# Chunked delta rule with two heads in one TensorE instruction, one Gram product for k and q, and transposed 16-blocks brought by transfer

## The chip, the cores and the metric

The kernel runs on one core of a Trainium2 chip. The metric is the device time of one execution in microseconds (us); several runs give a median.

## The reference

```python
# q, k, v: (4, 8, 768, 48) fp32, beta: (4, 8, 768); 32 heads in all
k_n = k / (norm(k) + 1e-6)
for t in range(768):
    y[:, :, t] = einsum('bhd,bhde->bhe', q[:, :, t], state)
    v_old = einsum('bhde,bhd->bhe', state, kt)
    state = state + bt * einsum('bhd,bhe->bhde', kt, vt - v_old)
x = y.transpose(0, 2, 1, 3).reshape(3072, 384)
logits = x @ w_gate                      # 8 experts, the best one for each token
# softmax weight of that expert; each expert keeps its 80 heaviest tokens
out[tok] = gate_w[tok] * (relu(x[tok] @ w1[e]) @ w2[e])   # F = 1024, all fp32
```

## The kernel before

Time is cut into NC = 12 chunks of C = 64 steps. Within a chunk the recurrence is a triangular system: the Gram matrix of the normalized k, masked and scaled by beta, gives `B1`; its inverse is built from 16x16 blocks (solved on POOL by `solve`) that `merge_*` joins to 32 and then 64. The 32 heads are named by e (0, 1), p (0, 1) and g (0 to 7).

A loop over j from -4 to 11 is a software pipeline written out by hand: an iteration works on chunk j+4 (scaling k), j+3 (transposes, Gram products, `fetch`, `solve`), j+2 (`spread`, `merge_y16`, `merge_p2`), j+1 (the other merges) and j (the chain over the state: `chain_ks`, `chain_tr`, `chain_qs`, `chain_ku`, `chain_pu`, then `out_t` and `logits`). The order of the calls in the loop is the order on every engine and on every DMA queue. `fill(n)` puts n small VectorE instructions (Newton steps of the norm, the gate, the top 80) between.

PE products of 32 heads go through `tiles` and `mm`: each head is its own product on a 64x64 quarter of the array, and the order goes round the four quarters. In fp32 each product is two LDWEIGHTS/MATMUL pairs in the trace, so such a product of all heads is 64 pairs. Three PSUM buffers (`mtile`, two banks each) go round; `S_ps` holds the state for the whole loop.

`gram_k` leaves `B1`, which goes to `a_blocks` in DRAM and comes back (`fetch`) as diagonal 16-blocks, one block to a partition, for `solve`. Its result goes to `inv_blocks` and comes back through `spread` in eight small DMAs into `xe`. `merge_y16` transposes it on PE by a product with `eye`. The DMA of `a_blocks` and `fetch` are issued from ACT's queue, all others of the loop from SP's.

After the loop come the routing (threshold, ranks, lists of tokens) and the experts: for each of 8 experts a gather of 80 rows, products at L803 and L811, and a scatter. The expert weights are loaded after the loop.

Of the kernel before, what the change touches and what calls it, by code (L numbers as in the profile page):

```python
# [24 lines left out]
def kernel(  # L25
# [49 lines left out]
    i_dram = [nc.dram_tensor(f"inv_blocks{i}", (128, 256), F32, kind="Internal") for i in range(2)]  # L75
# [61 lines left out]
    beta_t = keep.tile([128, NC, 2, NQ], F32, name="beta_t")  # L137
    beta_u = keep.tile([128, NC, 2, NQ], F32, name="beta_u")
# [18 lines left out]
    with ExitStack() as actx:  # L157
# [19 lines left out]
        KTs, QTs, PTs, B1s, Y16s, P2s, Ys, NTs, bms, Xss, xs = ({} for _ in range(11))  # L177
        St = [None]
# [7 lines left out]
        def sq4(t):  # L186
            return t.rearrange("r b (g w) -> r b g w", w=64)

        def d48(t):
            return t[:, :, : NQ * D].rearrange("r b (g d) -> r b g d", d=D)  # L190

        def halves(fn):
            for n in range(2):
                fn(slice(4 * n, 4 * n + 4))

        def wide(m):
            return m.unsqueeze(1).unsqueeze(1).to_broadcast([128, 2, 4, 64])

        def row(g):
            return g // 2 % 2  # L200

        def grp(g):
            return g // 4 * 2 + g % 2

        HEADS = [(e, p, g) for e in range(2) for p in range(2) for g in range(NQ)]

        def tiles(where, emit):

            cls = {}
            for hd in HEADS:  # L210
                cls.setdefault(where(*hd), []).append(hd)
            order = [kk for kk in ((0, 0), (1, 1), (0, 1), (1, 0)) if kk in cls]
            for n in range(max(len(x) for x in cls.values())):
                for kk in order:
                    if n < len(cls[kk]):
                        emit(*cls[kk][n])

        def mm(out, lhsT, rhs, acc=False):
            if acc:
                nc.tensor.matmul(out, lhsT=lhsT, rhs=rhs, start=False, stop=False, skip_group_check=True)  # L220
            else:
                nc.tensor.matmul(out, lhsT=lhsT, rhs=rhs, start=True, stop=True)  # L222
# [13 lines left out]
        def load_k(c):  # L236
            if ok(c):
                kr[c] = inp.tile([128, NB, D], F32, name="kr", bufs=4)
# [10 lines left out]
        def load_v(c):  # L249
            if ok(c):  # L250
                vin[c] = inp.tile([128, 2, NQ, D], F32, name="vin")
                src = vf.rearrange("(q p e) (c t) d -> p e c t q d", p=2, e=2, t=C)
                for p in range(2):
                    for e in range(2):
                        nc.sync.dma_start(vin[c][hs(e ^ p), p], src[p, e, c])
# [46 lines left out]
        def beta_mask(c):  # L302
            if ok(c):
                bms[c] = mat.tile([128, 2, NQ, 64], F32, name="bm", bufs=2)
                nc.gpsimd.tensor_tensor(out=bms[c].rearrange("r p g w -> r (p g) w"),
                                        in0=beta_t[:, c].rearrange("r p g -> r (p g)").unsqueeze(2).to_broadcast([128, NB, 64]),
                                        in1=neg_strict.unsqueeze(1).to_broadcast([128, NB, 64]), op=Alu.mult)

        def trans(dst, src):
            pt = mtile()  # L310
            for g in range(NQ):
                nc.tensor.transpose(pt[:, g // 4, (g % 4) * 128 : (g % 4) * 128 + 128],  # L312
                                    src[:, 2 * g : 2 * g + 2, :].rearrange("r p d -> r (p d)"), ident)
            for n in range(2):
                nc.scalar.copy(dst[:, 4 * n : 4 * n + 4], pt[:, n].rearrange("r (g w) -> r g w", w=128))  # L315

        def trans_k(c):
            if ok(c):
                KTs[c] = mat.tile([128, NQ, 128], F32, name="KT")
                trans(KTs[c], kn[c % NKB])  # L320

        def trans_q(c):
            if ok(c):
                QTs[c] = mat.tile([128, NQ, 128], F32, name="QT")
                trans(QTs[c], qn[c % NQB])

        def gram(dst, KT, r, mul):
            ps = mtile()
            tiles(lambda e, p, g: (p, e),
                  lambda e, p, g: mm(ps[hs(e), p, 64 * g : 64 * g + 64], KT[hs(p, D), g, hs(e)], r[hs(p, D), g, hs(e)]))  # L330
            halves(lambda s: nc.vector.tensor_tensor(out=dst[:, :, s], in0=sq4(ps)[:, :, s], in1=mul(s), op=Alu.mult))  # L331

        def gram_k(c):
            if ok(c):
                B1 = B1s[c] = mat.tile([128, 2, NQ, 64], F32, name="B1")
                bm = bms.pop(c)
                gram(B1, KTs[c], KTs[c], lambda s: bm[:, :, s])
                ad = a_dram[c % 2].rearrange("(e g z) -> e g z", e=2, g=NB)
                for e in range(2):
                    nc.scalar.dma_start(ad[e, :, : 64 * 64].rearrange("g (r w) -> r g w", w=64),  # L340
                                        B1[hs(e)].rearrange("r p g w -> r (p g) w"))

        def gram_q(c):
            if ok(c):
                PTs[c] = mat.tile([128, 2, NQ, 64], F32, name="PT")
                gram(PTs[c], KTs[c], QTs[c], lambda s: wide(strict))
# [7 lines left out]
        def solve(c):  # L354
# [3 lines left out]
            X = Xss[c] = sml.tile([128, 16, 16], F32, name="Xs")  # L358
            nc.gpsimd.tensor_tensor(out=X, in0=NT.rearrange("p s t -> p t s"), in1=eye16, op=Alu.add)  # L359
            for t in range(14, 0, -1):  # L360
# [5 lines left out]
                nc.gpsimd.tensor_tensor(out=X[:, t + 1 :, 0:t], in0=X[:, t + 1 :, 0:t], in1=tv, op=Alu.add)  # L366

        def spread(c):
            if not ok(c):
                return  # L370
            nc.sync.dma_start(i_dram[c % 2][:, :], Xss.pop(c).rearrange("p c s -> p (c s)"))
            src = i_dram[c % 2].rearrange("(e g i) (c s) -> e i c g s", e=2, i=4, s=16)
            dst = xe[c % 2].rearrange("r p g w -> r (p g) w")
            for e in range(2):
                for i in range(4):
                    nc.sync.dma_start(dst[64 * e + 16 * i : 64 * e + 16 * i + 16, :, 16 * i : 16 * i + 16], src[e, i])

# [465 lines left out]
```

## Time and profile before

| | |
|---|---|
| three runs | 557.03 us median, 550.74 to 561.35 |
| profiled execution | 548.66 us, its span 546.6 us |
| mean granted TensorE clock | 0.824 |
| busy shares | PE 69%, PEld 60%, DVE 38%, ACT 22%, POOL 32% |

The profile is of one execution. Engines are PE (matmul), PEld (weight load, overlaps PE), DVE, ACT, POOL; SPq and ACTq are the queues from which DMAs are issued. In groups of instructions, "busy" is the time in which at least one instruction of the group ran, so busy time over count is the pace of a stream, while "mean ns of one" holds the latency of each and is longer. A wait put down to "issue" is one in which the engine waited for nothing that the profile shows.

### The profile page before, as it was taken

How to read it: one execution, taken by the hardware profiler on the slowest of the kernel's cores; microseconds unless marked ns; L12 is line 12 of the kernel's file. 1: busy time of each engine (PE TensorE's matmuls, PEld its weight loads, DVE VectorE, ACT ScalarE, POOL GpSimd, SP SyncE). 2: the span in 40 equal slices, each digit the busy share in tenths (PEclk: the TensorE clock that was granted, in tenths of full speed). 3: DMA queues.
4: the chain of work that ended last, by engine and by line, in shares of the span. 5: the costliest groups of instructions: out<-in, count | busy, mean ns of one | idle time of the engine just before them, and what ended most of it. 6: DMA issues, size and time to landing. Idle time of an engine off the chain costs nothing. (4 is left out here: it accounts for less than half of the span.)

```text
span 546.6 us, 24604 instructions
## 1 busy us (share of the span) xinstructions
PE 379.9 (69%) x11259; PEld 327.2 (60%) x11271; DVE 209.9 (38%) x557; ACT 121.4 (22%) x218; POOL 177.0 (32%) x464
## 2 busy tenths in 40 slices
PE   2454768787787767678878868787500139999996
PEld 2343657676766657567768757776400028787673
DVE  4551244222532456323565523365285820101010
ACT  2021333222423223222322333223100000000000
POOL 7458374426171526317171515110020050010010
PEclk9999797778788797878786897787855555999999
DMA  9665557545372816435362534131386982782000
GB/s 159 93 104 86 100 101 124 103 83 131 59 157 53 147 34 130 89 68 114 55 135 34 117 62 102 24 92 27 83 326 227 387 288 96 268 287 89 10 9 19
DMA packets 173063, 63.84 MB, mean 117 GB/s; under 512 B 155008, under 2 KB 167808, under 8 KB 172960
## 3 DMA queue, kind: packets, MB, share of 16 engines
q1 hardware_dynamic: 122016, 52.33, 39.1%
q10 hardware_dynamic: 50176, 7.98, 8.6%
q0 software_dynamic: 768, 1.97, 1.2%
q8 instruction: 88, 1.44, 1.1%
q14 instruction: 15, 0.12, 0.1%
HBM read 43.95 MB, written 18.28 MB: 114 GB/s over the span
## 5 line engine op out<-in xcount | busy, mean ns | idle before, releaser
L222 PE MATMUL pm<-Y,P 64*64 64x64 f32 x1536 | 49.7, 247 | 5.5 <-issue 5.4
L222 PEld LDWEIGHTS pm<-Y,P 64*64 64x64 f32 x1536 | 46.3, 161 | 9.2 <-issue 7.5
L364 POOL TENSOR_TENSOR tmp<-Xs,NT 128x14 f32<-128x14 f32 (+6 forms) x168 | 47.5, 283 | 13.2
L803 PEld LDWEIGHTS hp<-xTe,w 128*128 128x128 f32 x384 | 48.9, 209 | 2.5 <-issue 1.2
L366 POOL TENSOR_TENSOR Xs<-Xs,tmp 128x14 f32<-128x14 f32 (+6 forms) x168 | 45.0, 268 | 13.2
L803 PE MATMUL hp<-xTe,w 128*128 128x80 f32 x384 | 48.9, 293 | 0.1
L299 POOL TENSOR_TENSOR kn<-kr,inv 128x768 f32<-128x768 f32 x12 | 18.4, 1531 | 84.3 <-PE S_ps L220 81.3
L811 PE MATMUL yp<-w,hT 128*80 128x384 f32 x128 | 44.3, 501 | 0.0
L806 ACT ACTIVATE hT<-hp 128x320 f32<-128x320 f32 x16 | 7.0, 437 | 135.0 <-PE hp L803 135.0
L815 POOL DMA_INDIRECT out_dram<-y,idx_s x8 | 7.4, 920 | 85.1 <-DVE y L814 85.1
L359 POOL TENSOR_TENSOR Xs<-NT,eye 128x256 f32<-128x256 f32 x12 | 10.2, 850 | 72.7 <-DMA NT<-a_blocks 72.7
L461 DVE TENSOR_TENSOR U<-pm,beta_u 128x384 f32<-128x384 f32 x24 | 12.3, 552 | 53.6 <-PE pm L222 53.6
L811 PEld LDWEIGHTS yp<-w,hT 128*80 128x80 f32 x128 | 19.2, 156 | 20.4 <-issue 20.4
L331 DVE TENSOR_TENSOR PT<-pm,strict 128x512 f32<-128x512 f32 x24 | 15.4, 685 | 40.6 <-PE pm L222 40.6
L222 PE MATMUL pm<-U,PT 64*64 64x48 f32 x768 | 19.0, 246 | 14.6 <-issue 13.9
L315 ACT COPY KT<-pm 128x512 f32<-128x512 f32 x24 | 12.9, 589 | 71.4 <-PE pm L312 71.4
L394 DVE TENSOR_TENSOR P<-pm,mask 128x512 f32<-128x512 f32 x24 | 15.5, 686 | 31.6 <-PE pm L220 31.6
L410 ACT COPY Y<-pm 128x512 f32<-128x512 f32 x24 | 12.9, 589 | 62.8 <-PE pm L222 16.5
L814 DVE TENSOR_SCALAR y<-yp,gw_t 80x384 f32<-80x384 f32 x8 | 4.9, 614 | 55.5 <-PE yp L811 55.5
L222 PEld LDWEIGHTS pm<-U,PT 64*64 64x64 f32 x768 | 16.4, 158 | 16.3 <-issue 14.9
L222 PE MATMUL pm<-KT 48*64 48x64 f32 x768 | 20.4, 270 | 7.1 <-issue 5.7
L222 PEld LDWEIGHTS pm<-KT 48*64 48x64 f32 x768 | 18.7, 183 | 8.3 <-issue 6.2
(168 smaller groups left out, 725.6 us busy)
## 6 DMA issues: line engine op xcount, KB each, us to landing
w<-in_moe_w_dram SPq DMA_DIRECT2D x16, 1536.0 KB, 8.7
a_blocks<-B ACTq DMA_DIRECT2D x24, 256.0 KB, 4.7
vin<-in_v_dram SPq DMA_DIRECT2D x52, 96.0 KB, 4.0
kr<-in_k_dram SPq DMA_DIRECT2D x24, 192.0 KB, 4.0
qn<-in_q_dram SPq DMA_DIRECT2D x24, 192.0 KB, 5.4
x_rows<-x SPq DMA_DIRECT2D x24, 192.0 KB, 3.1
out_dram<-zero SPq DMA_DIRECT2D x12, 384.0 KB, 3.2
NT<-a_blocks ACTq DMA_DIRECT2D x12, 128.0 KB, 2.9
```

Of the source, the lines that this page charges most:

```text
L222: nc.tensor.matmul(out, lhsT=lhsT, rhs=rhs, start=True, stop=True)
L299: nc.gpsimd.tensor_tensor(out=kn[c % NKB][:, :, 0:D], in0=kr.pop(c), in1=inv.pop(c).unsqueeze(2).to_broadcast([128, NB, D]), op=Alu.mult)
L315: nc.scalar.copy(dst[:, 4 * n : 4 * n + 4], pt[:, n].rearrange("r (g w) -> r g w", w=128))
L331: halves(lambda s: nc.vector.tensor_tensor(out=dst[:, :, s], in0=sq4(ps)[:, :, s], in1=mul(s), op=Alu.mult))
L359: nc.gpsimd.tensor_tensor(out=X, in0=NT.rearrange("p s t -> p t s"), in1=eye16, op=Alu.add)
L364: nc.gpsimd.tensor_tensor(out=tv, in0=X[:, t + 1 :, t : t + 1].to_broadcast(sh), in1=NT[:, 0:t, t].unsqueeze(1).to_broadcast(sh), op=Alu.mult)
L366: nc.gpsimd.tensor_tensor(out=X[:, t + 1 :, 0:t], in0=X[:, t + 1 :, 0:t], in1=tv, op=Alu.add)
L394: halves(lambda s: nc.vector.tensor_tensor(out=P2[:, :, s], in0=sq4(ps)[:, :, s], in1=wide(mask), op=Alu.mult))
L410: halves(lambda s: nc.scalar.copy(Y4[:, :, s], sq4(ps)[:, :, s]))
L461: halves(lambda s: nc.vector.tensor_tensor(out=U[:, :, s], in0=d48(ps)[:, :, s], in1=beta_u[:, c, :, s].unsqueeze(3).to_broadcast([128, 2, ...
L803: nc.tensor.matmul(hp[:, (f - f0) * cap : (f - f0 + 1) * cap], lhsT=w1_t[:, c, f * 128 : (f + 1) * 128], rhs=xTs[e][:, c, :], start=(c == ...
L811: nc.tensor.matmul(yp[:cap, :DM], lhsT=hT[:, f, :], rhs=w2_t[:, f, :], start=(f == 0), stop=(f == FK - 1))
```

## The change

The heads are re-paired. Six products (`chain_ks`, `chain_qs`, `chain_ku`, `chain_pu`, `merge_p2`, `merge_y4`) take two heads in one instruction: the left sides of two heads are stacked on 128 partitions, the right side is a block-diagonal tile that holds both heads (`SB`, `UB`, `XB`, `YB`, zeroed once), and the two results stand side by side. Such a product is 32 pairs, of 128 rows, 64 weight columns (48 in `chain_ku`) and 128 or 96 moving columns, on the two column halves of the array in turn. `gram_k` and `gram_q` become one product with k^T as weights and k^T and q^T side by side as the moving side (64 pairs of 128 columns). `merge_y16` is gone: POOL writes the transposed blocks beside the blocks, and eight more small DMAs (`spread_t`, four from SP's queue, four from ACT's) bring them into `YB`. `chain_qs` and `chain_pu` accumulate in one PSUM tile, which ACT copies out; the DVE addition is gone. `vin` comes in two DMAs in place of four. `logits` uses 64 columns of weights in place of 32 (24 pairs in place of 48). `merge_y5` now goes round four quarters of the array in place of two. `kn` has five buffers in place of four, and the loop's order changes. The core of the diff:

```diff
-        NKB, NQB = 4, 2
+        NKB, NQB = 5, 2
...
-        xe = [blk.tile([128, 2, NQ, 64], F32, name=f"xe{i}") for i in range(2)]
+        XB = blk.tile([128, NB, 2, 64], F32, name="XB")
+        YB = blk.tile([128, NB, 2, 64], F32, name="YB")
+        SB = blk.tile([128, NQ, 2, 2, D], F32, name="SB")
+        UB = blk.tile([128, NB, 2, D], F32, name="UB")
...
+        PAIRS = [(a, 4 * c + ql) for a in range(2) for ql in range(4) for c in range(2)]
+        XPAIRS = [(a, 4 * c + 2 * r + q) for a in range(2) for c in range(2) for q in range(2) for r in range(2)]
...
+        def gram(c):
...
+            for h in range(2):
+                ps = mtile()
+                tiles(lambda e, p, g: (p, e),
+                      lambda e, p, g: mm(ps[hs(e), p, 128 * (g % 4) : 128 * (g % 4) + 128].rearrange("r (k w) -> r k w", k=2),
+                                         KQ[hs(p, D), g, 0, hs(e)], KQ[hs(p, D), g, :, hs(e)]),
+                      [hd for hd in HEADS if hd[2] // 4 == h])
...
+                nc.vector.tensor_tensor(out=own(B1), in0=pv[:, 0], in1=own(bm), op=Alu.mult)
+                nc.vector.tensor_tensor(out=own(PT), in0=pv[:, 1], in1=strict.unsqueeze(1).to_broadcast([128, 8, 64]), op=Alu.mult)
...
+            nc.gpsimd.tensor_copy(XY[:, 1], X.rearrange("p t s -> p s t"))
...
+        def spread_t(c, q):
...
+                    if h == q:
+                        eng = (nc.sync, nc.scalar)[q]
+                        eng.dma_start(YB[r : r + 16, :, h, 16 * i : 16 * i + 16], src[h, i, 1])
...
+                for p, g in PAIRS:
+                    mm(ps[hs(g // 4), p, 128 * (g % 4) : 128 * (g % 4) + 128].rearrange("r (e w) -> r e w", e=2),
+                       B1[:, slot(p, g)], XB[:, slot(p, g)], acc=True)
...
+                            mm(ps[hs(p), e, 128 * ql : 128 * ql + 128].rearrange("r (c w) -> r c w", c=2),
+                               P2[:, p, ql, e], YB[:, 8 * e + 4 * p + ql])
...
+                for e, g in PAIRS:
+                    mm(ps[hs(g // 4), e, 2 * D * (g % 4) : 2 * D * (g % 4) + 2 * D].rearrange("r (p d) -> r p d", p=2),
+                       KQ[:, g, 0, hs(e)], SB[:, g, e])
...
+                for e, g in XPAIRS:
+                    mm(pxs[c][hs(g % 4 // 2), g // 4, 4 * D * (g % 2) : 4 * D * (g % 2) + 4 * D]
+                       .rearrange("r (p e d) -> r e p d", p=2, e=2)[:, e], KQ[:, g, 1, hs(e)], SB[:, g, e],
+                       acc=e + g % 2 > 0)
...
+                        mm(S_ps[hs(p, D), g // 4, 2 * D * (g % 4) : 2 * D * (g % 4) + 2 * D].rearrange("r (e d) -> r e d", e=2),
+                           kb[:, 2 * g + p, 0:D], UB[:, slot(p, g)], acc=True)
...
+                mm(ps[hs(g % 4 // 2), g // 4, o : o + 2 * D].rearrange("r (e d) -> r e d", e=2), PT[:, slot(p, g)], UB[:, slot(p, g)],
+                   acc=c > 0)
...
         for j in range(-4, NC):
-            beta_mask(j + 4)
             spread(j + 2)
             chain_ks(j)
-            fill(3)
-            trans_k(j + 3)
-            chain_qs(j)
             if j % 2 == 0:
                 bs = squares([j + 5, j + 6])
                 fillers.insert(0, newton(bs))
+            gram(j + 3)
             merge_x4(j + 1)
+            fetch(j + 3)
             chain_tr(j)
-            gram_k(j + 3)
-            fill(3 if j > -3 else 40 if j == -3 else 0)
+            fill(40 if j == -3 else 0)
             merge_y4(j + 1)
+            merge_p5(j + 1)
+            chain_qs(j)
             chain_ku(j)
             scale_k(j + 4)
-            merge_p5(j + 1)
-            fetch(j + 3)
-            fill(3)
+            beta_mask(j + 4)
             if j % GC == 1 and j > GC:
                 gate_pool(j // GC - 1)
             solve(j + 3)
             chain_pu(j)
-            fill(14)
-            trans_q(j + 3)
+            fill(20)
             load_k(j + 7)
             load_q(j + 5)
             load_v(j + 2)
+            spread_t(j + 2, 0)
             if 0 <= j < zr.shape[0]:
                 nc.sync.dma_start(zr[j], zero)
             merge_y5(j + 1)
+            trans(j + 4, 0, kn[(j + 4) % NKB])
+            trans(j + 4, 1, qn[(j + 4) % NQB])
             out_t(j)
-            gram_q(j + 3)
-            fill(6)
-            merge_y16(j + 2)
+            spread_t(j + 2, 1)
+            fill(10)
             merge_p2(j + 2)
-            fill(4)
             logits(j)
```

## Rows read from the trace of the kernel before

**Rows 1.** Busy time by stretch; the last iterations, all after the loop, the loop

```profile
core 0: us, PE busy (x) PEld busy (x) DVE busy (x) ACT busy (x) POOL busy (x), PEclk, DMA share, GB/s
...
336.40:358.50 22.10, 17.89 (x835) 16.57 (x828) 9.51 (x28) 6.66 (x13) 6.14 (x21) 0.85 0.22 49
358.50:382.40 23.90, 18.38 (x756) 16.82 (x748) 14.62 (x48) 6.76 (x13) 1.54 (x5) 0.79 0.24 59
382.40:394.00 11.60, 6.94 (x310) 6.01 (x310) 3.17 (x6) 1.67 (x4) 0.00 (x0) 0.90 0.20 61
394.00:546.60 152.60, 97.57 (x612) 72.73 (x612) 42.69 (x122) 7.74 (x17) 18.53 (x30) 0.77 0.52 183
93.90:394.00 300.10, 230.45 (x9111) 208.55 (x9113) 129.28 (x342) 89.08 (x161) 103.82 (x287) 0.82 0.43 86
```

**Rows 2.** Timeline of ACT: the copy in out_t, chunks 0 and 8

```profile
93.88 0.82 ACT L497 COPY xT<-pm 128x768 f32<-128x768 f32 x1
...
336.35 0.82 ACT L497 COPY xT<-pm 128x768 f32<-128x768 f32 x1
```

**Rows 3.** Waits of PE, 93.9 to 394 us: total, times, longest

```profile
PE pm L222 <- issue: 41.1, 30, 2.9
```

**Rows 4.** The page: busy us and instructions; DMA queues with packets, MB, share

```profile
PE 379.9 (69%) x11259; PEld 327.2 (60%) x11271; DVE 209.9 (38%) x557; ACT 121.4 (22%) x218; POOL 177.0 (32%) x464
...
q8 instruction: 88, 1.44, 1.1%
```

**Rows 5.** Timeline of PE in chunk 10's iteration: start, us, instructions

```profile
371.73 0.70 PE L220 MATMUL S_ps<-U,kn 64*48 64x48 f32 x47
373.79 0.40 PE L220 MATMUL S_ps<-U,kn 64*48 64x48 f32 x17 [1.36 <-issue]
374.12 0.75 PE L222 MATMUL pm<-X,B 32*32 32x32 f32 x64
374.80 0.91 PE L222 MATMUL pm<-U,PT 64*64 64x48 f32 x47
377.53 0.45 PE L222 MATMUL pm<-U,PT 64*64 64x48 f32 x17 [1.82 <-issue]
...
381.29 0.88 PE L495 MATMUL pm<-ident,x 128*128 128x128 f32 x6
```

**Rows 6.** Timeline of PE and all engines: gram_q, logits, merge_y5 at full clock

```profile
216.32 1.16 PE L222 MATMUL pm<-QT,KT 48*64 48x64 f32 x64
...
222.10 0.59 PE L505 MATMUL pm<-wg,xT 128*32 128x8 f32 x48
...
244.52 2.20 PE L222 MATMUL pm<-Y,P 64*64 64x64 f32 x64
```

**Rows 7.** Busy time by stretch, with the granted clock (columns as Rows 1)

```profile
216.30:217.40 1.10, 1.10 (x66) 1.07 (x65) 1.01 (x4) 1.10 (x2) 0.86 (x4) 1.00 1.15 218
222.10:222.60 0.50, 0.50 (x53) 0.49 (x48) 0.38 (x1) 0.00 (x0) 0.42 (x3) 1.00 1.05 290
```

**Rows 8.** Groups of instructions: the expert products

```profile
L803 PE MATMUL hp<-xTe,w 128*128 128x80 f32 x384 | 48.9, 293 | 0.1
L811 PE MATMUL yp<-w,hT 128*80 128x384 f32 x128 | 44.3, 501 | 0.0
```

**Rows 9.** Timeline of SP's queue, chunk 5's iteration

```profile
226.26 13.64 SPq L376 DMA_DIRECT2D xe<-inv_blocks  x8
243.74 1.25 SPq L487 DMA_DIRECT2D x_rows<-x  x2
245.10 1.39 SPq L247 DMA_DIRECT2D qn<-in_q_dram  x2
```

**Rows 10.** DMA issues: queue, count, KB each, median us to landing

```profile
a_blocks<-B ACTq DMA_DIRECT2D x24, 256.0 KB, 4.7
...
xe<-inv_blocks SPq DMA_DIRECT2D x96, 16.0 KB, 2.1
```

**Rows 11.** Groups of instructions on POOL, whole span

```profile
L359 POOL TENSOR_TENSOR Xs<-NT,eye 128x256 f32<-128x256 f32 x12 | 10.2, 850 | 72.7 <-DMA NT<-a_blocks 72.7
```

**Rows 12.** Waits of SP's queue, 123.8 to 308.3 us: total, times, longest

```profile
SPq L376 <- DMA a_blocks<-B: 16.2, 2, 8.8
```

More of the change, by code (lines that the diff above doesn't have):

```diff
@@ L184, in hs, with pq, slot, tiles @@
             return slice(64 * h, 64 * h + n)
[L186 to L203, printed above, removed]
+        def pq(p, g):
+            return 4 * p + g % 4
+        def slot(p, g):
+            return 2 * pq(p, g) + g // 4
         HEADS = [(e, p, g) for e in range(2) for p in range(2) for g in range(NQ)]
-        def tiles(where, emit):
+        PAIRS = [(a, 4 * c + ql) for a in range(2) for ql in range(4) for c in range(2)]
+        XPAIRS = [(a, 4 * c + 2 * r + q) for a in range(2) for c in range(2) for q in range(2) for r in range(2)]
+        def tiles(where, emit, heads=HEADS):
             cls = {}
-            for hd in HEADS:
+            for hd in heads:
                 cls.setdefault(where(*hd), []).append(hd)
@@ L218, in mm @@
         def mm(out, lhsT, rhs, acc=False):
[L219 to L222, printed above, removed]
+            nc.tensor.matmul(out, lhsT=lhsT, rhs=rhs, start=not acc, stop=not acc, skip_group_check=True)
         def mtile():
@@ L250, in load_v @@
             if ok(c):
[L251 to L255, printed above, removed]
+                vin[c] = inp.tile([128, NB, D], F32, name="vin")
+                src = vf.rearrange("(b g) (c t) d -> b c t g d", b=2, t=C)
+                for b in range(2):
+                    nc.sync.dma_start(vin[c][hs(b)], src[b, c])
         def squares(bs):
@@ L317, in trans_k @@
-        def trans_k(c):
-            if ok(c):
[L319 to L331, printed above, removed]
@@ L396, in merge_x4 @@
+                P2 = P2s[c] = one.tile([128, 2, 4, 2, 64], F32, name="P2")
+                for p in range(2):
+                    nc.vector.tensor_tensor(out=P2[:, p].rearrange("r g e w -> r (g e) w"), in0=ps[:, p].rearrange("r (g w) -> r g w", w=64),
+                                            in1=mask.unsqueeze(1).to_broadcast([128, 8, 64]), op=Alu.mult)
         def merge_x4(c):
             if ok(c):
-                ps, Y16, P2 = mtile(), Y16s[c], P2s[c]
-                tiles(lambda e, p, g: (p, e),
-                      lambda e, p, g: mm(ps[hs(e), p, 64 * g : 64 * g + 32], Y16[hs(p), e, g], P2[hs(p), e, g, 0:32]))
@@ L401, in merge_x4 @@
-                X4s[c] = one.tile([128, 2, NQ, 32], F32, name="X4")
-                nc.scalar.copy(X4s[c], sq4(ps)[:, :, :, 0:32])
+                ps, P2 = mtile(), P2s[c]
+                tiles(lambda e, p, g: (g // 4, e),
+                      lambda e, p, g: mm(ps[hs(e), g // 4, 32 * pq(p, g) : 32 * pq(p, g) + 32],
+                                         YB[hs(g // 4), 8 * e + pq(p, g), g // 4], P2[hs(g // 4), p, g % 4, e, 0:32]))
+                X4s[c] = one.tile([128, 2, 8, 32], F32, name="X4")
@@ L409, in merge_y4, with pos @@
                 Y4 = Y4s[c] = one.tile([128, 2, NQ, 64], F32, name="Y4")
-                halves(lambda s: nc.scalar.copy(Y4[:, :, s], sq4(ps)[:, :, s]))
+                for e in range(2):
+                    nc.scalar.copy(Y4[:, e], ps[:, e].rearrange("r (g w) -> r g w", w=64))
+        def pos(g):
+            return 2 * (g % 4) + g // 4
         def merge_p5(c):
@@ L424, in merge_y5 @@
                 ps, Y4 = mtile(), Y4s.pop(c)
-                tiles(lambda e, p, g: (e ^ p, e ^ p),
-                      lambda e, p, g: mm(ps[hs(e ^ p), p, 64 * g : 64 * g + 64], P5[hs(e ^ p), e, g], Y4[hs(e ^ p), p, g]))
-                Y = Ys[c] = one.tile([128, 2, NQ, 64], F32, name="Y")
-                halves(lambda s: nc.scalar.copy(Y[:, :, s], sq4(ps)[:, :, s]))
-        X4s, Y4s, Rs, Us = {}, {}, {}, {}
+                tiles(lambda e, p, g: (p, g // 4),
+                      lambda e, p, g: mm(ps[hs(g // 4), p, 64 * (4 * e + g % 4) : 64 * (4 * e + g % 4) + 64],
+                                         P5[hs(p), e, pos(g)], Y4[hs(p), e, pos(g)]))
+                Y = Ys[c] = one.tile([128, 2, 8, 64], F32, name="Y")
+                for p in range(2):
+                    nc.scalar.copy(Y[:, p], ps[:, p].rearrange("r (g w) -> r g w", w=64))
+        X4s, Y4s, Ys, Rs = {}, {}, {}, {}
         def chain_ks(c):
@@ L473, in chain_pu @@
+                for p in range(2):
+                    nc.scalar.copy(SB[hs(p, D), :, :, p].rearrange("r (b g) e d -> r b (g e) d", b=2),
+                                   S_ps[hs(p, D), :, : 8 * D].rearrange("r b (g d) -> r b g d", d=D))
         def chain_pu(c):
@@ L611 @@
             nc.vector.memset(t[:, :, D:], 0.0)
-        for t in xe:
+        for t in (XB, YB, SB, UB):
             nc.gpsimd.memset(t, 0.0)
```

185 lines of the change are left out of this document (85 added, 100 removed).

## The prediction

> **What bounds the kernel now.** I read the busy time by stretch first, cut at the copy of `out_t`, which runs once in each iteration from chunk 0 on. From chunk 0 to chunk 8 it moves from 93.88 to 336.35 us [rows 2], so eight steady iterations take 242.5 us, 30.3 each; the last three take 22.1, 23.9 and 11.6, and 152.6 us follow the loop, which the change leaves alone [rows 1]. In the 300.1 us of these iterations PE is busy 230.45, more than any other engine (DVE 129.28, POOL 103.82, ACT 89.08), and idle 69.7 [rows 1]. So the question is what the idle time waits for. The list of PE's waits says: nothing that the profile shows. The largest entry is 41.1 us of "issue" in 30 pieces, none over 2.9 us [rows 3].
>
> The timeline of PE shows what these pieces are. Between the pause that ends at 373.79 and the one that ends at 377.53 stand 17 + 64 + 47 = 128 pairs, that is 256 instructions, and no wait for another engine [rows 5]. The instruction queue moved 88 packets and 1.44 MB, 16 KB each [rows 4], and PE and PEld ran 22,530 instructions: 256 to a packet. So PE runs out of instructions at each 256 and waits for the next packet. There the period is 3.74 us for 128 pairs, of which about 1.9 is execution; when 128 pairs take longer than that, the pause vanishes. An iteration with everything in it has 904 pairs (13 products of 64, 16 + 6 transposes, 48 of `logits`, 2 of `merge_p2`), 7.06 packets, 26.4 us at this period. I conclude that instruction supply sets 26 of the 30 us.
>
> **What the change does to the supply.** Six products go from 64 to 32 pairs (-192), the two Gram products to one (-64), `merge_y16` goes (-64), `logits` halves (-24): 904 - 344 = 560 pairs, 4.4 packets, 16.4 us at 3.74. That no longer binds if the array needs longer.
>
> **What it does to the array.** The trace of before has no fp32 pair with 128 rows and 64 weight columns, so I bound its price by the expert rows [rows 8]. 128 pairs with 384 moving columns keep PE busy 44.3 us, 346 ns a pair, 0.90 ns a column. 384 pairs with 80 columns and 128 weight columns take 48.9/384 = 127 ns; 80 columns are 72, so 55 ns go to 128 weight columns, 28 ns to 64. A pair with 128 moving columns is then 115 + 28 = 143 ns on its own and one with 96 columns 114. If the two column halves of the array overlap fully, the pace is 115/2 = 58 and 86/2 = 43 ns; if not at all, 143 and 114. The nearest rows for the overlap are `logits` and `merge_y5`. `logits` has weights on all 128 rows and 32 columns, goes round four column strips, and makes 48 pairs in 0.59 us, 12 ns a pair [rows 6] at full clock [rows 7]; alone such a pair would be 14 + 7 = 21 ns. So column strips do overlap. `merge_y5`, on two quarters, makes 64 pairs of 64 columns in 2.20 us, 34 ns [rows 6], against 58/2 = 29 by the full overlap: 5 ns more. I take 58 + 5 and 43 + 5, so 2.0 us for each of `merge_p2` and `merge_y4`, 1.54 for each of the other four: 10.2 us in all. Before they took about 1.16 each, the pace of 64 pairs at full clock [rows 6, 7]: 7.0.
>
> [...]
>
> The rest of a new iteration at full clock: merged Gram, 64 pairs of 128 columns on four quarters, 115/4 + 4 = 33 ns, 2.1 us; `merge_x4`, `chain_tr` and `merge_y5` (now on four quarters) 3 x 1.16 = 3.5; `merge_p5` 0.75 and 22 transposes at 0.88/6 = 0.15, 3.2 [rows 5]; `logits` and the two pairs of `merge_p2` at most 0.9. Sum 20.6 us; neighbours start about 0.07 before the last one ends (374.12 + 0.75 against 374.80 in [rows 5]), over some 15 products 1 us: 19.6. So the array's own work stays what it was, and the gain is the pauses alone. The granted clock, 0.82 of full over the loop [rows 1], should rise to about 0.95 with fewer pauses: 20.5 us.
>
> **What is late next.** Two loops run close behind. (1) SP's queue. `spread_t` for `YB` stands behind `x_rows`, which waits for `chain_pu` and now for ACT's copy; `merge_x4` of the next iteration waits for `YB`, single-buffered. From `merge_x4` to the end of `chain_pu` PE needs 1.16 + 1.16 + 2.0 + 0.75 + 3 x 1.54 = 9.7 us. ACT's copies of state and x lie behind, some 2 us by estimate. Then SP issues `x_rows` 1.25, k, q and v at about 1.39 a pair of DMAs, and four DMAs of 16 KB, which I put at 0.5 each: 7.4. The last lands 2.1 later [rows 9, 10]. Sum 21 us, just above the array. (2) `fetch` moves forward on ACT, so ACT stands still until `a_blocks` has landed, 4.7 us after issue [rows 10]; behind it are the copies of `merge_y4`, `merge_p5` and the state. By the order of PE their users come 5 us or more later, so I cost it at 0; if that cover is gone it costs the wait, up to 4.7. POOL is busy 103.82 us for some eight full solves [rows 1], 13 an iteration, plus 0.85 for the transposed copy [rows 11]; hidden below 20. DVE gets wider evacuations of U but loses the addition of x and half of v's work stays; hidden too, except where the gate's small instructions bunch.
>
> **The sum.** Taking 1 to 1.5 us for waits that don't overlap, a steady iteration is 22 us: 8 x (30.3 - 22) = 66 off. The last three lose the same share of pairs but run on fewer products; I take 17, 15.5 and 10.5 for 22.1, 23.9 and 11.6: 14.6 off. Chunk 0's own iteration has the same pauses, about 5 off. Before it the pipeline is filled by latency (norm, transposes, `a_blocks`, solve, spread), where the first Gram product now waits for q too, each solve has its copy and POOL clears four larger tiles: I allow 4 more, from nothing to 8. Total -82: from the profiled 548.66 to 467. The median of the runs shown is 557.03, 1.5% above the profiled one; I forecast the median, 472.
>
> **Rivals.** (a) Column halves don't overlap, so stacked pairs cost 143 and 114 ns. The six take 2 x 4.6 + 4 x 3.65 = 23.8 us and not 10.2: an iteration of 35.6, eight of them +42, the last three about +15: 57 more, some 614 us, slower. It decides as soon as a pair costs more than about 110 ns with 128 columns and 90 with 96. [...] Against it: `logits` at 12 ns. 8%. (b) SP's queue becomes the bound. In the profile eight spread DMAs once took 13.64 us to issue [rows 9] where 8 x 0.5 would do, because one stood behind a transfer of another queue [rows 12]; the change has 29 DMAs an iteration where there were 23. If one such delay of 5 us falls in each iteration, it is 27 us: 512 us. 18%. (c) The supply doesn't follow the count, or its pauses are replaced by waits for evacuation (three PSUM buffers, and one of them now held from `chain_qs` to `chain_pu`): an iteration of 29 to 30 and about 550 us. Against it: the pauses come every 128 pairs whatever product runs. 8%. (d) Waits overlap and the stacked pairs run at the full-overlap price, 58 and 43 ns, 9.2 us for the six: an iteration of 18.5 to 19, about 446 us. 10%.
>
> **How the numbers follow.** My forecast, an iteration of 20.5 to 24.5, has 56% and 458 to 494 us. The range of 440 to 522 takes in (b), most of (d), and leaves out (a), (c) and the ends, about 18%. Two per cent, about 11 us, is what a measurement of this kernel can tell from no change. Faster by more than that: the forecast, (b), (d) and a little of (c), 0.85; within it 0.06; slower, (a) and the ends of (c), 0.09.
>
> **What would show it.** In the profile after: about 7,100 pairs in place of 11,260, with the instruction queue at 56 packets or so; the total of PE's "issue" in the loop at a third or less of before; stacked pairs at 55 to 65 ns (128 columns) and 45 to 50 (96), that is 32 pairs of `merge_y4` in about 2.0 us; the copies of `out_t` 20 to 24 us apart; the mean clock in the loop above 0.9; and 152 us after the loop as before. Waits of PE for a DMA into `YB` or `XB` would point to (b), waits for copies out of PSUM to (c), a stream of stacked pairs above 100 ns to (a).

## The result and the profile after

The changed kernel takes 512.06 us (median of 4 runs, 508.54 to 516.41) against 558.33 for the kernel before beside it (4 runs): ratio 0.922, 95% interval 0.905 to 0.940. It is faster, towards the slow end of the range; the gain is 46 us where 85 were forecast (472 for 557). The profiled execution took 510.11, its span is 508.1 and its mean granted clock 0.844.

Each part is measured at the places of [rows 1, 2]. The start of the copy of `out_t` (now line 501), from the timeline of ACT, cuts the span; the times between are:

| stretch | before | forecast | after | after less forecast |
|---|---|---|---|---|
| to the copy of chunk 0 | 93.9 | 92.9 (fill +4, chunk 0 -5) | 99.4 | +6.5 |
| eight iterations | 242.5 | 176 | 204.2 | +28.2 |
| last three | 57.6 | 43 | 53.4 | +10.4 |
| after the loop | 152.6 | 152.6 | 151.1 | -1.5 |

The last column adds up to 43.6, close to the 43.1 by which the profiled 510.11 lies above the 467 of the sum. Most of the miss is in the eight iterations: 25.5 us where 22 stood.

Busy time by stretch, after (columns as Rows 1: length, then PE, PEld, DVE, ACT, POOL, granted clock, DMA share, GB/s); first the eight iterations, then the last three, then all after the loop:

```profile
99.43:303.58 204.15, 164.09 (x4458) 153.85 (x4466) 104.19 (x254) 69.19 (x122) 97.92 (x254) 0.89 0.60 117
303.58:324.46 20.88, 16.52 (x479) 15.62 (x480) 8.83 (x28) 6.42 (x12) 8.16 (x27) 0.92 0.39 85
324.46:345.28 20.82, 16.42 (x479) 15.39 (x479) 10.38 (x32) 6.40 (x12) 1.54 (x5) 0.92 0.30 67
345.28:357.00 11.72, 7.63 (x190) 6.58 (x190) 6.91 (x20) 1.68 (x5) 1.39 (x7) 1.00 0.23 69
357.00:508.10 151.10, 97.25 (x588) 72.64 (x588) 42.65 (x122) 7.79 (x17) 17.21 (x23) 0.78 0.53 185
```

PE is busy 20.5 us of an iteration (164.09/8), as forecast, but idle 5.0. Before, by [rows 1, 2], it was busy 23.4 and idle 6.9. So of the 38 us that the eight iterations gained, 23 are shorter busy time, at a granted clock of 0.89 in place of 0.82, and only 15 are idle time. What is PE still idle for? The page's lines on engines and on the instruction queue, after:

```profile
PE 354.1 (70%) x7227; PEld 311.8 (61%) x7239; DVE 213.2 (42%) x545; ACT 117.5 (23%) x207; POOL 190.6 (38%) x476
...
q8 instruction: 57, 0.93, 0.8%
```

The waits of PE, after, 94 to 400 us (total, times, longest):

```profile
PE pm L207 <- DMA YB<-inv_blocks: 28.5, 7, 5.6
PE tb_ps L720 <- DVE thrw L718: 28.0, 1, 28.0
PE pm L590 <- DVE ohg L569: 12.0, 2, 6.2
PE pm L207 <- DVE lg L511: 6.8, 4, 4.9
PE pm L207 <- issue: 5.0, 6, 1.2
...
PE S_ps L207 <- issue: 0.7, 1, 0.7
```

[rows 3] has only the largest of the entries of "issue" before. The others, 93.9 to 394 us:

```profile
PE S_ps L220 <- issue: 7.3, 7, 2.1
PE pm L505 <- issue: 7.2, 5, 2.1
PE pm L220 <- issue: 5.1, 3, 2.1
```

So there are 57 packets in place of 88, and 5.7 us of "issue" in place of 60.7. Nearly all of the pauses are gone, as forecast. (`thrw` lies after the loop.) In their place stand a transfer into `YB` and two results of DVE: `ohg`, the last result of the gate, and `lg`, the copy of the product of `logits` out of PSUM.

The timeline of PE, after, shows both on the way from chunk 4 to chunk 6 (start, us, instructions, idle before and what ended it):

```profile
206.47 0.82 PE L509 MATMUL pm<-wg,xT 128*64 128x8 f32 x24
207.14 1.52 PE L207 MATMUL pm<-SB,KQ 128*64 128x96 f32 x32
213.53 3.69 PE L207 MATMUL pm<-KQ 48*64 48x128 f32 x64 [4.88 <-DVE lg L511]
...
220.25 1.97 PE L207 MATMUL pm<-YB,P 128*64 128x128 f32 x32
...
235.38 1.98 PE L207 MATMUL pm<-KQ 48*64 48x128 f32 x64
240.65 1.94 PE L207 MATMUL pm<-P,YB 64*64 64x32 f32 x61 [3.29 <-DMA YB<-inv_blocks]
...
242.47 1.70 PE L207 MATMUL pm<-R,Y 64*64 64x48 f32 x63
```

Stacked pairs cost what was forecast: 1.97/32 = 62 ns with 128 moving columns, 1.52/32 = 48 with 96. The Gram product `pm<-KQ` takes 1.98 us (granted clock 1.00 from 235.38 to 237.36 us), or 3.69 behind the wait of 4.88 (0.50 from 213.5 to 217.3): the wait is paid a second time, at the lower clock. The windows around another wait of the after kernel, the one of 4.18 us for `YB` at 307.7, show it (same columns):

```profile
307.70:311.80 4.10, 0.00 (x0) 0.00 (x0) 1.02 (x2) 0.00 (x0) 3.24 (x12) 1.00 0.54 131
311.90:315.50 3.60, 3.60 (x128) 3.57 (x128) 0.00 (x0) 0.59 (x1) 0.84 (x2) 0.53 0.23 81
315.60:319.40 3.80, 3.80 (x127) 3.59 (x128) 2.00 (x3) 1.65 (x3) 0.00 (x0) 1.00 0.16 22
```

Right after the idle stretch the granted clock is 0.53 of full for the 3.6 us of `merge_x4` and `chain_tr`; from 315.6 us on it is 1.00 again.

**The loop through `YB`.** It is read from two timelines, after, one round of it. PE:

```profile
110.25 1.95 PE L207 MATMUL pm<-P,YB 64*64 64x32 f32 x61 [5.01 <-DMA YB<-inv_blocks]
...
134.65 2.08 PE L207 MATMUL pm<-P,YB 64*64 64x32 f32 x61 [4.01 <-DMA YB<-inv_blocks]
```

SP's queue:

```profile
122.04 1.25 SPq L491 DMA_DIRECT2D x_rows<-x  x2
123.39 1.38 SPq L226 DMA_DIRECT2D kr<-in_k_dram  x2
124.82 1.83 SPq L232 DMA_DIRECT2D qn<-in_q_dram  x2
126.98 3.36 SPq L239 DMA_DIRECT2D vin<-in_v_dram  x2
130.44 2.09 SPq L367 DMA_DIRECT2D YB<-inv_blocks  x4
```

From `merge_x4` (`pm<-P,YB`) to `x_rows` 11.8 us (forecast 9.7 + 2), from `x_rows` to the end of the issues for `YB` 10.5 (forecast 7.4), from there to the next `merge_x4` 2.1 (forecast 2.1): 24.4 us where 21 was put. PE then waits for it. The middle part is the one that is longer than put, and so it is in all five rounds from chunk 0 on that load k, q and v: 10.5 to 11.7 us.

**The block on DVE.** The timeline of DVE, after, ahead of the wait of 4.88 us: from 203.50 to 212.10 it holds ten rounds of a maximum and a replacement (`gate_top`), 0.86 us each, of which the last stands here. The `fill(10)` of the new order draws them, ahead of `merge_p2`:

```profile
211.25 0.37 DVE L597 MAX8 cand<-cand 48x8 f32<-48x208 f32 x1
211.66 0.08 DVE L598 MATCH_VALUE_LOAD cand<-cand,cand 48x8 f32 x1
211.74 0.35 DVE L598 MATCH_REPLACE8 cand<-cand,cand 48x208 f32<-48x208 f32 x1
212.10 1.29 DVE L380 TENSOR_TENSOR P<-pm,mask 128x512 f32<-128x512 f32 x2
213.31 0.17 DVE L511 COPY lg<-pm 128x16 f32<-128x16 f32 x1
```

The evacuations of `merge_p2` (L380) and `logits` (L511), products that were done by 207.3, stand behind the block; the wait of PE ends with the copy into `lg`.

### The profile page after: what moved, and what is told of

It is laid out like the page before. It is cut to its first block, busy times and chain, and to the rows that moved or that the text cites. A ratio compares the mean times of both kernels' runs of the same rounds, so it can differ in the third digit from the quotient of the medians.

```text
span 508.1 us, 16641 instructions
## 1 busy us (share of the span) xinstructions
PE 354.1 (70%) x7227; PEld 311.8 (61%) x7239; DVE 213.2 (42%) x545; ACT 117.5 (23%) x207; POOL 190.6 (38%) x476
## 3 DMA queue, kind: packets, MB, share of 16 engines
q10 hardware_dynamic: 63232, 8.77, 10.5%
q0 software_dynamic: 768, 1.97, 1.3%
## 5 line engine op out<-in xcount | busy, mean ns | idle before, releaser
L343 POOL TENSOR_TENSOR tmp<-XY,NT 128x14 f32<-128x14 f32 (+6 forms) x168 | 48.2, 287 | 13.2
L345 POOL TENSOR_TENSOR XY<-XY,tmp 128x14 f32<-128x14 f32 (+6 forms) x168 | 45.8, 273 | 13.2
L207 PE MATMUL pm<-P,YB 64*64 64x32 f32 x768 | 22.7, 279 | 37.7 <-DMA YB<-inv_blocks 35.8
L453 DVE TENSOR_TENSOR UB<-pm,beta_t 64x768 f32<-64x768 f32 x24 | 22.9, 955 | 60.2 <-PE pm L207 59.9
L207 PE MATMUL pm<-KQ 48*64 48x128 f32 x768 | 29.2, 311 | 12.7 <-ACT KQ L301 7.1
L380 DVE TENSOR_TENSOR P<-pm,mask 128x512 f32<-128x512 f32 x24 | 15.5, 686 | 49.4 <-PE pm L207 49.4
L207 PE MATMUL pm<-SB,KQ 128*64 128x96 f32 x704 | 35.0, 254 | 1.2 <-DVE lg L511 1.2
L207 PEld LDWEIGHTS pm<-KQ 48*64 48x64 f32 x768 | 25.8, 157 | 14.8 <-ACT KQ L301 7.8
L301 ACT COPY KQ<-pm 128x512 f32<-128x512 f32 x48 | 24.9, 613 | 34.8 <-PE pm L298 24.3
L207 PEld LDWEIGHTS pm<-SB,KQ 128*64 128x64 f32 x704 | 31.2, 141 | 2.2 <-PE pm L590 1.5
L207 PE MATMUL pm<-XB,B 128*64 128x128 f32 x384 | 25.3, 288 | 6.2 <-DMA YB<-inv_blocks 3.9
```

The lines of the kernel that those rows point to most:

```text
L207: nc.tensor.matmul(out, lhsT=lhsT, rhs=rhs, start=not acc, stop=not acc, skip_group_check=True)
L301: nc.scalar.copy(KQs[c][:, 4 * h : 4 * h + 4, n, :], pt[:, h].rearrange("r (g w) -> r g w", w=128))
L343: nc.gpsimd.tensor_tensor(out=tv, in0=X[:, t + 1 :, t : t + 1].to_broadcast(sh), in1=NT[:, 0:t, t].unsqueeze(1).to_broadcast(sh), op=Alu.mult)
L380: nc.vector.tensor_tensor(out=P2[:, p].rearrange("r g e w -> r (g e) w"), in0=ps[:, p].rearrange("r (g w) -> r g w", w=64), in1=mask.unsqu ...
L453: nc.vector.tensor_tensor(out=UB[hs(e), :, e].rearrange("r (g c) d -> r c g d", c=2), in0=ps[hs(e), :, : 8 * D].rearrange("r c (g d) -> r ...
```

## The experiments

Theory: the pauses of the supply are gone, and the time now goes to two waits, the loop through SP's queue and `YB`, and the gate's block on DVE, each made dearer by the clock behind it. Rivals: the supply still sets the pace (its packets only came to overlap other waits), or the stacked pairs do. The median of before, run beside each, was 556.38 us for e1 and e3 to e5, 554.69 for e6 to e8, 554.96 for e9 and e10, and 557.66 for e11; the changed kernel's own was 558.33. So differences of 2 or 3 us between kernels of different groups say nothing.

**e4_before_pad, e5_after_pad: the supply.** The same 128 tiny pairs, 256 instructions and so one packet (the instruction queue has 99 packets in e4, 88 before), are added to each of 11 iterations of either kernel, ahead of `chain_ku`'s product (they add to columns of the state's PSUM tile that nothing reads):

```diff
+        def pad():
+            for n in range(128):
+                q = 32 * (n % 4)
+                nc.tensor.matmul(S_ps[q : q + 32, 1, 496:504], lhsT=identb[:, q : q + 32], rhs=eyes[:, 0, 0:8],
+                                 start=False, stop=False, skip_group_check=True)
...
+                pad()
```

> The kernel before with 128 tiny pairs of 8 bf16 columns added in each of eleven iterations, written to columns that nothing reads. Theory (instruction supply bounds the kernel before, 256 instructions per 3.4 to 4.4 us): each iteration grows by one packet, 11 x 3.4 to 4.4, so 37 to 48 us more than before, some 600 us. Rival (the array's own time bounds it): 128 pairs at the 12 ns of logits, 1.5 us an iteration, 17 us more, some 574 us.

> The changed kernel with the same 128 tiny pairs in each of eleven iterations. Theory (supply no longer binds; each iteration has room of 25 us for 4.4 packets): it costs the array's time at most, 1.5 us an iteration on the loop through YB, so 10 to 17 us more than the changed kernel, 520 to 530. Rival (supply still binds): 37 to 48 us more, 550 to 560.

Before with the pairs: 598.72 us (595.9 to 600.71), ratio 1.078 (1.072 to 1.083), 42 more than before, 3.8 an iteration. After with them: 535.49 (534.2 to 537.65), ratio 0.962 (0.957 to 0.968), 23 more than after. In the kernel before the price is a full period of the supply, 3.74 us in [rows 5], although the 128 pairs take only 1.30 us in e4 where no pause falls among them: the supply set its pace. In the changed kernel they cost 2.1 an iteration, between both expectations. Most groups of them in e5 have a pause among them, and they stand on the loop through `YB`, so their time shows. The timeline of PE in e5:

```profile
239.42 0.69 PE L470 MATMUL S_ps<-eyes,identb 128*32 128x8 bf16 x70
241.12 0.58 PE L470 MATMUL S_ps<-eyes,identb 128*32 128x8 bf16 x58 [1.01 <-issue]
```

PE's "issue" in e5, 90 to 400 us, adds up to 19.7 us in 16 pieces, against 5.7 in 7 in the changed kernel. So some 14 of the 23 us stand in the trace as pauses of the supply: it is no longer the bound of the whole, but near enough to come back.

**e1_yb_early: the place on SP's queue.** The four DMAs move ahead of the wait for x:

```diff
             merge_y4(j + 1)
+            spread_t(j + 2, 0)
...
             load_v(j + 2)
-            spread_t(j + 2, 0)
```

> The changed kernel with SP's four YB transfers issued right behind merge_y4, ahead of x_rows and the loads; nothing else differs. Theory (the loop over SP's queue sets the iteration: merge_x4, the chain, x_rows, the loads, YB, merge_x4): PE's wait for YB, 39.7 us in nine pieces, falls below 15, steady iterations go from 25.5 to about 22 us, the time from 512 to 475 to 490. Rival (YB waits because DMA engines or the chain from gram to solve are late, whatever the place in the queue): the wait moves to XB or to gram and the time stays at 505 to 515.

491.26 us (488.57 to 494.32), ratio 0.883 (0.877 to 0.889): 21 below after, just above the range of the theory. The waits of PE in e1, 90 to 400 us:

```profile
PE pm L590 <- DVE ohg L569: 10.7, 2, 6.2
PE pm L207 <- DMA YB<-inv_blocks: 10.0, 6, 3.7
PE pm L207 <- issue: 9.0, 8, 2.0
```

One line moved, nothing taken out: the wait for `YB` falls from 28.5 to 10.0 us and the time by 21. The place of `spread_t` behind `x_rows` was about half of the miss of 40 us. Five of the eight iterations are 21.0 to 23.4 us long now, three 26.0 to 27.3.

**e6_yb_by_pe: no DMAs into YB.** The transposed blocks are made by a product with `eye`, 64 pairs, as `merge_y16` did, and copied by ACT and DVE; the eight DMAs and POOL's copy are gone:

```diff
-            nc.gpsimd.tensor_copy(XY[:, 1], X.rearrange("p t s -> p s t"))
...
+            ps = mtile()
+            tiles(lambda e, p, g: (e, g // 4),
+                  lambda e, p, g: mm(ps[hs(g // 4), e, 64 * pq(p, g) : 64 * pq(p, g) + 64], XB[hs(e), slot(p, g), e], eye[hs(e)]))
+            for h, copy in ((0, nc.scalar.copy), (1, nc.vector.tensor_copy)):
+                copy(YB[hs(h), :, h].rearrange("r (e m) w -> r e m w", e=2), ps[hs(h)].rearrange("r e (m w) -> r e m w", w=64))
...
-            spread_t(j + 2, 0)
...
-            spread_t(j + 2, 1)
...
             fill(10)
+            merge_yb(j + 2)
```

> The changed kernel with one part undone: YB comes from a product with eye on PE (64 pairs of 64 columns) and two copies, as merge_y16 did, in place of POOL's copy and eight transfers. Theory (the loop through YB's transfers sets the changed kernel's iteration): the wait for YB goes, PE gains 1.2 us of work, steady iterations fall from 25.5 to 22 to 24 us, 475 to 495 us, about as with the early transfers. Rival (the transfers cost nothing, the iteration is bound by gram, solve and spread or by the array): PE's 64 pairs make it slower, 510 to 530.

487.61 us (485.48 to 490.7), ratio 0.877 (0.871 to 0.882). The 64 pairs that the change saved by transfer cost less than the transfer at its place: 24 below after. Six of its eight iterations are 21.6 to 23.5 us long, near the forecast's 22; two take 27.3 and 29.8.

**e7_warm: the clock behind a wait.** 48 pairs of bf16 work for nothing, between the Gram product and `merge_x4`, where PE waits for `YB`:

```diff
+        def warm():
+            for n in range(48):
+                nc.tensor.matmul(S_ps[:, 1, 400:512], lhsT=identb, rhs=eyes.rearrange("r g w -> r (g w)")[:, 0:112],
+                                 start=False, stop=False, skip_group_check=True)
...
+            if 0 <= j < NC - 1:
+                warm()
```

> The changed kernel with 48 pairs of 112 bf16 columns more in each of eleven iterations, between gram and merge_x4, where PE waits for YB 3 to 6 us; nothing reads their result. Theory (the wait halves TensorE's granted clock, and the products behind it, which lie in the loop through YB, then run at half pace): the added 3.5 us fit into the wait, the clock stays up, and the time falls or stays, 498 to 512. Rival (the clock costs nothing here, or added work is added time): 11 x 2 to 3.5 us more, 530 to 550.

504.37 us (501.28 to 513.63), ratio 0.906 (0.901 to 0.912): 8 below after, with more work. That is under 2%, and the intervals of the two ratios overlap (after: 0.905 to 0.940), so the gain is likely but not sure. The timeline of PE in e7 (its profiled execution took 513.63 us; only these neighbouring rows are read from it):

```profile
240.74 2.53 PE L385 MATMUL S_ps<-eyes,identb 128*128 128x112 bf16 x48
243.67 1.20 PE L207 MATMUL pm<-P,YB 64*64 64x32 f32 x61 [0.40 <-DMA YB<-inv_blocks]
```

The useless pairs fill the wait here, and `merge_x4` behind them takes 1.20 us in place of 1.94. Over the ten rounds of the trace it takes 1.9 us or more in one, against eight of ten after. That each round on the loop through `YB` gets shorter by it is argued, not shown: the profiled execution was no faster than that of the changed kernel.

**e3_one_half: the price of the stacked pairs without overlap.** `PAIRS` goes through one column half first and then the other, in the two products that use it (`merge_p2` and `chain_ks`):

```diff
-        PAIRS = [(a, 4 * c + ql) for a in range(2) for ql in range(4) for c in range(2)]
+        PAIRS = [(a, 4 * c + ql) for c in range(2) for a in range(2) for ql in range(4)]
```

> The changed kernel with merge_p2 and chain_ks in another order: all products of one column half of the array first, then those of the other. Theory (stacked pairs run at 62 and 48 ns because two column halves work at once): 32 pairs of merge_p2 take 4.0 to 4.6 us in place of 1.97, those of chain_ks 3.2 to 3.6 in place of 1.52; the others stay. Rival (halves don't work side by side, a stacked pair is simply cheaper): 1.97 and 1.52 as they are.

One run, 499.56 us. The timeline of PE in e3:

```profile
207.38 1.20 PE L207 MATMUL pm<-P,YB 64*64 64x32 f32 x61 [2.10 <-DMA YB<-inv_blocks]
...
208.43 1.15 PE L207 MATMUL pm<-R,Y 64*64 64x48 f32 x63
...
220.71 3.00 PE L207 MATMUL pm<-XB,B 128*64 128x128 f32 x29
...
224.56 2.37 PE L207 MATMUL pm<-SB,KQ 128*64 128x96 f32 x30
```

Two things follow. Pairs on one half cost 3.00/29 = 103 ns and 2.37/30 = 79 ns, less than the theory's 125 to 144 and 100 to 113; in turn on two halves they cost 62 and 48, so the halves overlap by a factor of 1.7. And the kernel with the slower pairs was faster in its one run, by some 12 us. The pairs lie outside the loop through `YB` and fill PE's wait for it, which falls from 28.5 to 12.0 us in all (2.10 here, and `merge_x4` behind it takes 1.20). So that they cost nothing is plain; that the clock is what made the kernel faster is argued from e7's like case, and one run does not show it.

**e8_all_sp: waits across queues.** In the changed kernel SP's queue waits for a DMA of ACT's queue that it doesn't read. The waits of SP's queue, after, 94 to 357 us:

```profile
SPq L351 <- DMA a_blocks<-B: 16.7, 5, 8.6
SPq L356 <- DMA a_blocks<-B: 7.2, 2, 6.3
```

L351 is the DMA to `inv_blocks`, L356 the eight DMAs into `XB`, both in `spread`. e8 is e6 with all these transfers on SP's queue, in the order of their use (`spread` is split into its two parts):

```diff
-                nc.scalar.dma_start(ad[e, :, : 64 * 64].rearrange("g (r w) -> r g w", w=64), B1[hs(e)])
+                nc.sync.dma_start(ad[e, :, : 64 * 64].rearrange("g (r w) -> r g w", w=64), B1[hs(e)])
...
-                nc.scalar.dma_start(NTs[c], a_dram[c % 2].rearrange("(s z) -> s z", z=PB)[:, :1024]
+                nc.sync.dma_start(NTs[c], a_dram[c % 2].rearrange("(s z) -> s z", z=PB)[:, :1024]
...
-            spread(j + 2)
...
-            merge_x4(j + 1)
+            spread(j + 2)
             fetch(j + 3)
+            spread_xb(j + 2)
+            merge_x4(j + 1)
```

> As the kernel with YB from PE, and a_blocks and fetch go to SP's queue, in the order a_blocks, inv_blocks, fetch, XB, so that no transfer of the loop is issued from ACT. Theory (once YB is out of the way, transfers of one queue wait for those of the other, and the next bound is gram, a_blocks, solve, XB): waits of SP for a_blocks that delay XB go, steady iterations 21 to 22.5 us, 465 to 482 us. Rival (SP is now so full that loads and x_rows come late): 490 to 510.

488.91 us (482.09 to 492.93), ratio 0.872 (0.865 to 0.880): no difference from e6 (0.871 to 0.882) that the runs can tell, and outside the 465 to 482 of the theory. Its trace still has iterations of 27.5 and 28.7 us. So those waits cost little once `YB` is off the queue, and the iterations of 27 to 30 us have another cause.

**e9_gate_late, e10_after_gate_late, e11_early_late: the gate's block.** The gate's product, its top 80 and POOL's part move to the end of the next iteration; `gate_top` is handed out in halves of a round, and the fills are smaller and in more places. e9 does that to e6, e10 to the changed kernel, e11 to e1:

```diff
                 nc.vector.max(m8, cd)
+                yield 1
...
-            if j % GC == 1 and j > GC:
-                gate_pool(j // GC - 1)
+            fill(8)
             solve(j + 3)
             chain_pu(j)
-            fill(20)
+            fill(12)
...
-            fill(10)
+            fill(6)
+            if j % GC == 1 and j > GC:
+                fill(100)
+                gate_pe(j // GC - 1)
+                fillers.append(gate_top(j // GC - 1))
+                gate_pool(j // GC - 1)
...
-            if j >= GC and j % GC == 0:
-                fill(100)
-                gate_pe(j // GC - 1)
-                fillers.append(gate_top(j // GC - 1))
```

> YB brought by a product on PE as in e6_yb_by_pe, and besides the gate's part (its logits product, top-1 and POOL work) is called at the end of the iteration after, spread in smaller fills over the following iteration. Theory (what is left over the forecast's 22 us an iteration is the gate's bunched DVE instructions: the iterations with them took 27 to 30 us where plain ones took 22 to 23.5, the copies of U and the products' results stand behind them): those iterations fall to 23 to 26 us, 470 to 480 us in all, 8 to 18 below e6's 488. Rival (DVE's small instructions are hidden and the long iterations come from the solve's transfers and the clock): no change, 485 to 492 us.

> The changed kernel with the gate's part alone moved as in e9_gate_late; the eight DMAs into YB stay. Theory (the loop through SP's queue and YB sets 24 to 25 us of each iteration, the gate's DVE work only what exceeds that): 500 to 508 us, 4 to 12 below the changed kernel's 512. Rival (the gate's instructions are the main delay, YB's wait a consequence): 485 to 498 us. Second rival (DVE is hidden altogether): 509 to 515 us.

> The changed kernel with both moves: spread_t's four DMAs of SP's queue behind merge_y4 as in e1_yb_early, the gate's part late as in e10_after_gate_late; no pair is added. Theory (two separate causes: e1 took 21 us off the changed kernel, e10 took 10): their sum, 476 to 486 us, iterations near 23 us throughout and the granted clock in the loop above 0.93. Rival (the two are one delay, the second move finds nothing left): 488 to 495 us.

| kernel | median (runs) | ratio to before | gate's move alone |
|---|---|---|---|
| e9: YB by PE, gate late | 478.60 (476.54 to 483.55) | 0.868 (0.859 to 0.876) | -9.0 against e6 |
| e10: gate late | 502.19 (500.75 to 503.34) | 0.907 (0.901 to 0.913) | -9.9 against after |
| e11: YB early, gate late | 478.57 (477.17 to 482.39) | 0.861 (0.854 to 0.867) | -12.7 against e1 |

All three lie where the theory put them. Of the three differences in the last column only that of e11 is clear of the intervals; the other two are under 2%. The two moves add up: -21 for the place of `spread_t`, -10 for the gate, -33 together. In e11 the three long iterations of e1 (27.2, 27.3 and 26.0 us) take 23.6, 23.6 and 20.9. Over the eight iterations the gate's move gains 9.3 us there, and 9.8 in e9. In e10 it gains only 4, as PE's wait for `YB` grows from 28.5 to 34.9 us; 3 more come ahead of chunk 0, where no gate runs and only the smaller fills differ. Busy time by stretch and waits of PE in e11 (94 to 280, and 90 to 400 us):

```profile
94.00:280.00 186.00, 163.12 (x4525) 148.44 (x4522) 101.87 (x254) 71.53 (x126) 103.08 (x274) 0.97 0.66 133
```

```profile
PE pm L207 <- issue: 11.2, 12, 2.0
PE pm L590 <- DVE ohg L569: 8.2, 1, 8.2
...
PE pm L207 <- DMA YB<-inv_blocks: 5.0, 3, 2.1
```

PE is busy 88% of the time at a clock of 0.97, and the copies of `out_t` are 20.9 to 23.9 us apart, 22.7 in the mean. e9 and e11 are 33 us below the changed kernel and 76 to 79 below the one before. What is left first is the supply again.

## Why the prediction was right, and where its size was off

1. **Supply as the bound of before: right.** Packets 88 to 57 (forecast 56), pairs 11,259 to 7,227 (some 7,100), "issue" 60.7 to 5.7. e4 shows it from the other side: one more packet an iteration costs 3.8 us, the period read in [rows 5]. Rival (c) is out in its first form and at its price; its second form, waits for evacuation, came in part: 6.8 us of PE's waits end with the copy into `lg` (see 5).
2. **Price of the stacked pairs: right.** 62 and 48 ns against 63 and 48. Rival (a) is out, and its own price was too high: without overlap 103 and 79 ns were measured in e3, not 143 and 114. One reason is the rows that it was worked out from. [rows 8] holds a first group of each product below full clock (10.53 us at 0.50 and 7.04 at 0.76); the seven others take 5.48 and 5.33 (1.00 from 466.69 to 482.70 us), that is 114 and 333 ns a pair, and the same working gives 133 and 106. What is left, 103 against 133 and 79 against 106, says that weight columns and moving columns don't simply add in these pairs. All of them stand on 128 rows, and e3 against the changed kernel shows the two column halves overlapping by the factor of 1.7. The row of `merge_y5` in [rows 6], from which the 5 ns beside the full overlap were put, is not at full clock: 0.94 was granted from 244.52 to 246.72 us, so some 2 of the 5 are the clock (an estimate, 34 x 0.06).
3. **The array's work: right.** PE is busy 20.5 us an iteration at a clock of 0.89, and in e11 19.9 at 0.97 (163.12/186 of 22.7); forecast 20.5 at 0.95. Busy time times clock, 19.2 us before and 18.3 after, is nearly the same, as the prediction says of the array's own work. But "the gain is the pauses alone" hides that 23 of the 38 us gained show as shorter busy time at the higher clock.
4. **What is late next: right in name, wrong in size, and this is the step that failed.** The loop (1) through SP's queue was put at 21 us and "just above the array"; it measured 24.4 in the round shown. The term that was mis-sized is `x_rows` to the last issue for `YB`: 7.4 forecast, 10.5 measured. The forecast took 1.39 us for each pair of loads; in this round q's took 1.83 and v's 3.36, and 0.6 went between the issues, while the four small DMAs took 2.09, near the 2.0 that was put. The trace of before already had longer ones, on SP's queue:

```profile
122.93 2.92 SPq L247 DMA_DIRECT2D qn<-in_q_dram  x2
125.90 4.20 SPq L255 DMA_DIRECT2D vin<-in_v_dram  x4
...
150.97 2.85 SPq L241 DMA_DIRECT2D kr<-in_k_dram  x2
```

This is rival (b)'s place, at part of its price (3 us an iteration, not 5). The range held because it took in (b); the forecast's own 458 to 494 did not hold. That the result falls on (b)'s 512 us is luck: the iterations took 25.5 us and not its 27, and the last three and the prologue (7, 8) make up the difference. A second thing that the sum lacks is the clock: behind the wait of 4.18 us `merge_x4` and `chain_tr`, which stand on the same loop, took 3.6 us at a granted clock of 0.53, where e3 has 1.20 + 1.15, and the changed kernel itself 1.12 + 1.16 at 1.00 (291.27 to 293.40 us). The 11.8 us from `merge_x4` to `x_rows` hold that already. e1 and e6 show the place; the clock rests on e7, with a gain under 2%.
5. **DVE "hidden, except where the gate's small instructions bunch": the exception came, and no number stood for it.** It is worth some 10 us once the wait for `YB` is gone (e9 and e11, with the smaller fills), and less in the changed kernel itself, where the two overlap (e10). The count that was overlooked stands in the diff: `fill(10)` ahead of `merge_p2`, ten rounds of 0.86 us, where the old order had `fill(6)` there and `fill(4)` behind.
6. **`fetch` at no cost on ACT: right as far as shown.** No copy of ACT behind it appears among PE's larger waits. Its DMAs hold up `inv_blocks` on SP's queue, but e8 shows no gain from taking that away.
7. **The last three iterations** stayed at 53.4 us where 43 stood. The trace has waits for `YB` there as well (7.6 us in two). Neither move alone shortens them (52.7 in e1, 52.8 in e10), both together do: 48.0 in e11 (19.6, 17.3, 11.0).
8. **The prologue** lost 5.5 us, within the 0 to 8 that were allowed, but chunk 0 didn't give its 5 back. Most of this is again the place of `spread_t`: in e1 chunk 0's copy stands at 94.5 us, and PE's waits for `YB` in the first 99.5 us fall from 11.2 to 5.0. PE's wait for `kn` from POOL grew from 6.1 to 16.6 us there, while that for the first q^T shrank; it is as long in e1, so it is not what cost the 5.5. Why it grew stays open; POOL's larger clears are only a guess.

With most of the waits of 4 and 5 taken away (e11), the steady iteration is 22.7 us against 22 forecast, and the kernel 478.6 against 472: the reasoning on supply and array carried, and the term for what is late next was too small. The step from the sum to the median is a small slip of its own: 467 and 1.5% are 474, not 472.

Open: why an iteration of e11 stays 2.8 us above PE's busy time (about half of that is supply), and how much of the gains of e3 and e7 is the clock.

## What to carry to other kernels

When the bound of a kernel is removed, write out the loop that is second as a sum of queue entries and give each entry the longest duration that the trace has for it; here the loop was 3 us too short an iteration, and moving four DMAs out of it gave back 21 of the 40 us that were missing (e1). A transfer that frees the array can cost more than the work that it saves when its issue stands behind a wait on its queue: in its first place it cost 24 us more than the product on PE (e6). In the better place it brought nothing over that product either: 491.3 against 487.6 (e1, e6), and 478.6 for both with the gate late (e11, e9). Small filler instructions cost PE time here where an evacuation stood behind them (PE's waits for the copy into `lg` are 0.8 us in the loop before, 6.8 after): count them by time (0.86 us each here), not by number.

## What was unexpected of the hardware

- A long wait of TensorE was paid twice here: the granted clock was 0.53 for the 3.6 us behind the one of 4.18. After waits of 3.29, 4.18 and 5.01 us `merge_x4` took 1.94 to 1.95 us for 61 pairs, after waits of 0.40 and 2.10 us 1.20. Between them either occurs: 1.95 after 2.70 us in e3, 1.20 after 2.98 us in e10, 1.95 after 0.61 us in e5, where the Gram product just ahead had taken 3.69 behind a wait of 2.47. The kernel with useless work in the wait (e7) was 8 us faster, which is under 2%.
- With slower instructions off the critical loop the kernel was faster in one run (e3, by 12 us); that it is by the same way is not shown.
- Stacked fp32 pairs on one column half cost 103 ns with 128 moving columns and 79 with 96, less than weight and moving columns cost when added from the expert rows at a granted clock of 1.00 (133 and 106).
